# Retention after softplus and squared-ReLU products: each tile's retention moved next to its use, the weights' sign taken on ScalarE, and another cut of the first product's tiles

## The chip, the cores and the metric

One core of a Trainium2 chip runs the whole program. The metric is device time in microseconds; the kernel before took 913.0 us (median of 3 runs, 912.48 to 913.43).

## What is computed

Retention (a masked, decayed product of scores with v), and on its output two feed-forward layers, the first with softplus, the second with a squared ReLU. All inputs and results are float32, and the weights come as float64.

```python
scores = scale * np.matmul(q, k.transpose(0, 1, 3, 2))        # batch 4, heads 8, sequence 576, head 64
ret = scores * Dmat[None]                                     # gamma ** (row - column), causal
x = np.matmul(ret, v)  ->  [2304 tokens, 512]
h = x @ w_in;  x = (np.maximum(h, 0) + np.log1p(np.exp(-np.abs(h)))) @ w_out    # 512 -> 2048 -> 512
h = x @ w_in2; out = np.maximum(h, 0) ** 2 @ w_out2                             # 512 -> 2048 -> 512
```

## The kernel before

Every float32 operand of the large products is split into two parts, hi and lo, and a product is three passes (hi by hi, hi by lo, lo by hi). So one step of a layer, 128 of its 2048 inner columns over one tile of tokens, is 12 matmuls of the first product (`g1`, line 336, tile `ph`) and 12 (in the second phase three per 128 tokens) of the second (`g2`, line 405, tile `acc`). A block is one tile of tokens, 16 steps; `g2` runs two steps behind `g1`. The first phase (softplus) has five blocks, whose lengths in tokens stand in `TILES` (line 25: 512 and four times 448); the second phase (squared ReLU) has five, in `TILES2` (line 26: 384, 512, 512, 512, 384). In the first phase the tokens are the moving columns of both products; in the second they are the moving columns of `g1` alone, and `g2` moves 512 weight columns.

Softplus per step: three ScalarE operations (lines 350 to 352) and three on VectorE (357, 360, 363), then the split of its result (383 on ScalarE, 384 on VectorE).

The weights are split on the chip, one item per 128 rows or columns of a weight matrix (`split_w`, lines 108 to 141): 32 items a phase. An item waits for its load (512 KB, lines 100 and 105, into one of three stages), takes two ScalarE operations (121, 122), a VectorE operation that isolates the sign (126), one that puts the words together (130, tile `ct`), a ScalarE copy to hi (138) and a VectorE subtraction to lo (139). `weights(j)` says how many items are to be through by step j: all 32 of the first phase within the 16 steps of block 0. The other 32 are split in blocks 4 and 5. `pump_step` runs one piece of an item's split, up to the next `yield`; while the first tile is prepared, each chunk calls it once.

The retention runs in 36 chunks of 64 tokens, every chunk a tick: scores and state (`step_s`, lines 237 and 243, then the mask on VectorE at 247 and a state copy on ScalarE at 249), and one tick later the output (`step_o`, line 259, then the decay weights on VectorE at 275). v is weighted on VectorE at line 222 (`scale_v`). The chunks are loaded four ahead (208, 212). Chunks 0 to 7 make the first tile before block 0 starts. The other 28 are spread evenly over the first 29 steps by `attend`, half a tick at the start and half at the end of a step. The output of chunks of tile 1 stays on chip in `x_raw`; that of later tiles goes to device memory (`x1d`, line 285) and comes back a block ahead (line 428). At the end of a block `split_x` (316 to 319) makes the next tile's hi and lo.

Only the start is ordered by hand (`manual_schedule`). After it the order of instructions on each engine comes from a planner that takes the program's order as priority and moves work that is ready ahead of work that waits. Loads and stores are all issued by SyncE's queue, in order.

Of the kernel before, what the change touches and what calls it, by code (L numbers as in the profile page):

```python
# [16 lines left out]
P = 128  # L17
D = 64
CN = 64  # tokens of a chunk of the retention
SCN = 9  # chunks of a sequence  # L20
LOADS = 4  # chunks on chip
STAGES = 3  # weights on chip as they come
XEND = 29  # steps of the first product that carry the retention
# Tiles of tokens of the two phases: start, length.
TILES = ((0, 512), (512, 448), (960, 448), (1408, 448), (1856, 448))
TILES2 = ((0, 384), (384, 512), (896, 512), (1408, 512), (1920, 384))
# Columns of the constants' array: 1 - 2^-23, 0.49, weights of v, the causal mask (the latter two in the
# lower half of the partitions), and weights of the output.
# [6 lines left out]
def kernel(  # L35
# [12 lines left out]
    """Products of float32 matrices as three passes: each operand is the exact sum of two parts  # L48
    that float32r holds, hi (rounded) and lo (the rest), and hi*hi, hi*lo and lo*hi are summed in
    PSUM; lo*lo lies below float32's last bit.  # L50

    Retention runs in chunks of 64 tokens, with every head in the free dimension. Two operands are
    stacked in the partitions: [q, transposed; masked scores] against [state; v] gives a chunk's
    output. With i counted from the sequence's start, v takes gamma^-i, and the output scale *
    gamma^i; the state, the sum of k * v over the chunks before, then grows in PSUM without decay.
    """
# [32 lines left out]
    x1d = [dram.tile([P, n // CN, KD, CN], F32, name=f"x1d{t}") for t, (_, n) in enumerate(TILES)]  # L89
    x2d = dram.tile([KD, P, NT], F32, name="x2d")  # L90

    # ---------------------------------------------------------------- weights
# [15 lines left out]
    def split_w(phase, kind, f):  # L108
        """The two words of each float64 to float32 hi and lo, in steps.

        2^-112 times the upper word, read as a float32, has float32's exponent in place of
        float64's (values below float32's range go to 0). Shifted by 3 bits, with the sign put back
        and with 3 bits for the lower word, it is the float32. The lower word's upper half is
        mapped to 0 to 7, which keeps the mean error at 0.
        """
        t = staged.pop((kind, f))
        y, up, low = t.bitcast(F32)[:, :, 1], t[:, :, 1], t[:, :, 0]
        ct = cvt.tile([P, DM], U32, tag="ct", name="ct")
        halves = t.bitcast(U16).rearrange("p a (b two) -> p a b two", two=2)
        half, sign = halves[:, :, 0, 1], halves[:, :, 1, 1]  # L120
        nc.scalar.activation(out=y, in_=y, func=AF.Copy, scale=2.0**-112)
        nc.scalar.activation(
            out=low, in_=half, func=AF.Identity, bias=round_up, scale=7.0 / 65535
        )
        yield
        nc.vector.tensor_scalar(  # L126
            out=half, in0=sign, scalar1=0x8000, scalar2=None, op0=ALU.bitwise_and
        )
        yield
        nc.vector.scalar_tensor_tensor(  # L130
            out=ct, in0=up, scalar=3, in1=low,
            op0=ALU.logical_shift_left, op1=ALU.bitwise_or,
        )
        yield
        y = ct.bitcast(F32)
        hi = wts.tile([P, DM], F32R, tag=f"{kind}h{f}", name=f"{kind}h{f}")
        lo = wts.tile([P, DM], F32R, tag=f"{kind}l{f}", name=f"{kind}l{f}")
        nc.scalar.copy(hi, y)
        nc.vector.tensor_tensor(out=lo, in0=y, in1=hi, op=ALU.subtract)  # L139
        w_hi[phase, kind, f], w_lo[phase, kind, f] = hi, lo  # L140
        yield True
# [19 lines left out]
    def pump_step():  # L161
        """A step of the next weights' split; loads others into the stage that a whole one frees."""
        if not splitting:
            m = n_split[0]
            if m == len(items):
                return
            pump_load(m + 1)
            splitting.append(split_w(items[m][0], items[m][2], items[m][3]))
            n_split[0] += 1
        if next(splitting[0]):  # L170
            splitting.clear()
            pump_load(n_split[0] + STAGES)

    def pump(count):
        """Splits the next weights."""
        for _ in range(count):
            while True:
                pump_step()
                if not splitting:
                    break  # L180

    # -------------------------------------------------------------- retention
# [45 lines left out]
    def step_s(c, split):  # L228
        """Scores of chunk c, with keys in the partitions, and the state after it."""
# [6 lines left out]
        for h in range(H):  # L236
            nc.tensor.matmul(  # L237
                pb[HI, h, :], lhsT=kk[LO, h, :], rhs=qp[LO, h, :],
                start=True, stop=True, skip_group_check=True,
            )  # L240
            if go_on:
                # One start clears what the whole bank held.
                nc.tensor.matmul(
                    st[LO, h, :], lhsT=kk[HI, h, :], rhs=sv[HI, h, :],
                    start=c % SCH == 0 and h == 0, stop=True, skip_group_check=True,
                )
# [4 lines left out]
    def step_o(c, ps):  # L251
# [16 lines left out]
        elif t == 1:  # L268
            if t not in x_raw:
                x_raw[t] = xs.tile([P, 512 // CN, KD, CN], F32, tag="xr", name="xr")  # L270
            x = x_raw[t][:, m]
        else:
            # In place of the chunk's keys, which nothing reads any more.
            x = qkv[:, 1, 0:KD, :]
        nc.vector.tensor_tensor(out=x, in0=po, in1=xw, op=ALU.mult)
        if t == 0:
            # Nothing reads the operands of a product yet.
# [6 lines left out]
        if t > 1:  # L284
            nc.sync.dma_start(out=x1d[t][:, m], in_=x)
# [3 lines left out]
    def tick_first(split=False):  # L289
        """Scores and state of chunk k."""  # L290
# [4 lines left out]
    def tick_second(ps_o, load=True):  # L295
        """Output of chunk k - 1; loads run ahead."""
# [7 lines left out]
    # ------------------------------------------------------------------ GEMMs  # L304
    def split_x(raw, phase, n):
        """raw -> a tile's operands of the first product."""
# [34 lines left out]
    def softplus_a(key, n):  # L341
        """e = exp(-|h|), ln(1 + e), and a bound of log1p(e) from below that is sharp for small e.

        1 + e is rounded, which spoils the logarithm of small e: it is taken a last bit lower, and
        e - e^2/2 takes over where that is more.
        """
# [76 lines left out]
    def load_x(phase, t0, n):  # L423
        raw = xs.tile([P, 512 * KD], F32, tag="xr", name="xr")
        if phase == 0:
            t, _ = tile_of(t0)
            raw = raw.rearrange("p (m a b) -> p m a b", a=KD, b=CN)
            nc.sync.dma_start(out=raw[:, :n // CN], in_=x1d[t])
        else:
            raw = raw.rearrange("p (a b) -> p a b", a=KD)  # L430
            nc.sync.dma_start(
                out=raw[:, :, :n], in_=x2d[:, :, t0:t0 + n].rearrange("k p n -> p k n")
            )
        return raw

    # --------------------------------------------------------------- schedule
# [3 lines left out]
    # Chunks that have to be through before each tile of the first phase.  # L440
# [9 lines left out]
    def keep_warm(count):  # L450
        """Products that nothing reads: TensorE's clock stays up while the operands come."""
# [36 lines left out]
    half = [0]  # L488
    rest = 2 * (NCH - need[0])

    def attend(j, h2):
        """Attention's half ticks, spread evenly over the first steps."""
        pos = 2 * j + h2 + 1
        want = min(rest, -(-rest * pos // (2 * XEND)))
        while half[0] < want:
            if half[0] % 2 == 0:
                tick_first()
            else:
                tick_second(ps_at)
                scale_v(tick[0] - 2 + LOADS)  # L500
            half[0] += 1

    def weights(j):
        """How many weights of the first phase are split by step j."""
# [10 lines left out]
    for j, (b, f) in enumerate(steps):  # L515
# [11 lines left out]
        attend(j, 0)  # L527
        if j >= 1:
            split_g(j - 1, blocks[steps[j - 1][0]][2])
        if ph == 0:  # L530
            pump(max(0, weights(j) - n_split[0]))
        if j >= 2:
# [5 lines left out]
        attend(j, 1)  # L538
# [8 lines left out]
        if f == KF - 1 and b + 1 < len(blocks):  # L547
            split_x(x_next[0] if b else x_raw.pop(1), blocks[b + 1][0], blocks[b + 1][2])
            if b + 2 < len(blocks):
                x_next[0] = load_x(*blocks[b + 2])  # L550
# [11 lines left out]
def _by_dims(a):  # L562
    """[B, H, S, D] -> chunk, dimension, head, token of the chunk."""
# [7 lines left out]
def _by_tokens(a):  # L571
    """[B, H, S, D] -> chunk, token of the chunk, head, dimension."""
# [7 lines left out]
def _constants(n_heads, head_dim):  # L580
    """Decay weights and the causal mask: they depend on shapes alone."""
# [48 lines left out]
```

## Time and profile before

| | |
|---|---|
| time, 3 runs | 912.48, 913.0, 913.43 us; median 913.0 us |
| profiled execution, span | 913.3 us (no other time of it is recorded) |
| TensorE matmul / weight load busy | 896.1 us (98%) / 765.7 us (84%) |
| VectorE, ScalarE, GpSimd busy | 517.6 (57%), 429.3 (47%), 12.3 us (1%) |
| mean granted TensorE clock | 0.992 of full speed |
| moved by DMA | 74.2 MB, 81 GB/s over the span |

Matmuls overlap, so a matmul's own duration in the trace is longer than its share of the time; what counts is the distance from one start to the next. The clock was full (1.00, that is 2.4 GHz) in every stretch after the start. Engines' busy shares are given by stretch below, since the stages have different limits.

### The profile page before, as it was taken

The page shows a single profiled execution, that of the slowest core. Times are in us where ns is not written, and L with a number is a line of the kernel's source. Part 1 is how long each engine was busy: PE and PEld are TensorE (multiplying, and loading weights), DVE is VectorE, ACT ScalarE, POOL GpSimd, SP SyncE. Part 2 cuts the span into 40 slices and gives each one's busy share as a digit, 9 for nine tenths or more (in the row PEclk, how much of TensorE's full clock was granted, in tenths as well). Part 3 has the DMA queues.
Part 4 walks back from the last instruction along what each step waited for, and adds up shares of the span by engine and source line. Part 5 has one row for each costly group of instructions (what it writes and reads, how often), then busy time and mean ns, then how long its engine had stood idle before and what let it go on. Part 6 is the DMA issues. An engine that isn't in the chain of part 4 may idle for free.

```text
span 913.3 us, 13514 instructions
## 1 busy us (share of the span) xinstructions
PE 896.1 (98%) x5478; PEld 765.7 (84%) x5478; DVE 517.6 (57%) x849; ACT 429.3 (47%) x751; POOL 12.3 (1%) x16
## 2 busy tenths in 40 slices
PE   7999999999999999999999999999999999999998
PEld 6876777788899999999999998888888888888997
DVE  2799999966555547456985799522332233223322
ACT  2588777643454455444875598322222222222222
POOL 2300000000000000000000000000000000000000
PEclk8899999999999999999999999999999999999999
DMA  9867577743111002001520465200020001000100
GB/s 247 202 168 234 163 217 206 216 119 88 42 47 41 0 1 81 1 1 36 179 93 0 156 206 164 81 1 0 1 93 1 1 22 59 1 1 1 46 1 35
DMA packets 39181, 74.20 MB, mean 81 GB/s; under 512 B 3280, under 2 KB 25552, under 8 KB 38992
## 3 DMA queue, kind: packets, MB, share of 16 engines
q1 hardware_dynamic: 39120, 73.35, 26.7%
q8 instruction: 43, 0.70, 0.3%
q14 instruction: 18, 0.15, 0.1%
HBM read 61.15 MB, written 12.19 MB: 80 GB/s over the span
## 4 chain that ended last, share of the span: by engine, by line
PE 77%; DVE 10%; DMA 8%; ACT 3%; issue 2%; SPq 0%; POOL 0%; POOLq 0%; ACTq 0%; DVEq 0%
PE acc L405 37%; PE ph L336 36%; DMA wi_raw<-in_moe_w_in_dram 4%; DVE ct L130 2%; DMA wo_raw<-in_moe_w_out_dram 2%; DMA ch<-in_kv_dram 1%; PE po L259 1%; PE st L237 1%; DVE wo_raw L126 1%; DVE wol L139 1%; DVE wil L139 1%; DVE gl L384 1%; PE cold L453 1%; DVE wi_raw L126 1%; DVE l L360 1%
## 5 line engine op out<-in xcount | busy, mean ns | idle before, releaser
L336 PE MATMUL ph<-xh,wih 128*128 128x512 f32 (+2 forms) x640 | 240.3, 376 | 1.3 <-ACT xh L279 0.4
L336 PE MATMUL ph<-xh,wil 128*128 128x512 f32 (+2 forms) x640 | 238.0, 372 | 0.3 <-DVE wil L139 0.3
L336 PE MATMUL ph<-xl,wih 128*128 128x512 f32 (+2 forms) x640 | 159.0, 370 | 0.0
L336 PEld LDWEIGHTS ph<-xh,wih 128*128 128x128 f32 x640 | 120.2, 188 | 20.2 <-DVE xh L318 1.0
L336 PEld LDWEIGHTS ph<-xh,wil 128*128 128x128 f32 x640 | 120.3, 188 | 16.0 <-DVE wil L139 0.8
L336 PEld LDWEIGHTS ph<-xl,wih 128*128 128x128 f32 x640 | 118.8, 188 | 14.8
L405 PE MATMUL acc<-gh,woh 128*128 128x448 f32 (+1 forms) x320 | 121.4, 381 | 0.0
L405 PE MATMUL acc<-gl,woh 128*128 128x448 f32 (+1 forms) x320 | 119.6, 374 | 0.3 <-DVE gl L384 0.2
L405 PE MATMUL acc<-gh,wol 128*128 128x448 f32 (+1 forms) x320 | 119.7, 374 | 0.0
L376 DVE TENSOR_TENSOR g<-r 128x512 f32<-128x512 f32 (+1 forms) x80 | 51.2, 639 | 114.3 <-ACT r L370 111.7
L405 PE MATMUL acc<-woh,gl 128*128 128x512 f32 x288 | 113.1, 393 | 1.0 <-DVE gl L384 1.0
L405 PE MATMUL acc<-wol,gh 128*128 128x512 f32 x288 | 112.7, 391 | 0.0
L405 PE MATMUL acc<-woh,gh 128*128 128x512 f32 x288 | 112.3, 390 | 0.0
L384 DVE TENSOR_TENSOR gl<-g,gh 128x512 fp32r<-128x512 f32 (+1 forms) x80 | 51.1, 639 | 102.0 <-ACT gh L383 102.0
L370 ACT ACTIVATE r<-ph 128x512 f32<-128x512 f32 (+1 forms) x80 | 44.2, 553 | 129.5 <-PE ph L336 129.5
L383 ACT CAST gh<-e 128x448 fp32r<-128x448 f32 (+1 forms) x80 | 46.0, 575 | 119.5 <-DVE e L363 117.2
L383 ACT CAST gh<-g 128x512 fp32r<-128x512 f32 (+1 forms) x80 | 46.3, 579 | 116.0 <-PE acc L405 107.1
L357 DVE SCALAR_TENSOR_TENSOR e<-e 128x448 f32<-128x448 f32 (+1 forms) x80 | 51.3, 641 | 65.7 <-ACT l L352 65.4
L384 DVE TENSOR_TENSOR gl<-e,gh 128x448 fp32r<-128x448 f32 (+1 forms) x80 | 51.1, 639 | 30.4 <-ACT gh L383 29.9
L405 PEld LDWEIGHTS acc<-gh,woh 128*128 128x128 f32 x320 | 60.1, 188 | 8.2
L405 PEld LDWEIGHTS acc<-gl,woh 128*128 128x128 f32 x320 | 60.1, 188 | 7.5 <-DVE gl L384 1.0
L405 PEld LDWEIGHTS acc<-gh,wol 128*128 128x128 f32 x320 | 60.1, 188 | 7.5
(52 smaller groups left out, 1068.9 us busy)
## 6 DMA issues: line engine op xcount, KB each, us to landing
wi_raw<-in_moe_w_in_dram SPq DMA_DIRECT2D x32, 512.0 KB, 4.6
wo_raw<-in_moe_w_out_dram SPq DMA_DIRECT2D x32, 512.0 KB, 3.9
ch<-in_qk_t_dram SPq DMA_DIRECT2D x36, 256.0 KB, 4.9
ch<-in_kv_dram SPq DMA_DIRECT2D x36, 256.0 KB, 5.4
out_dram<-xo SPq DMA_DIRECT2D x18, 256.0 KB, 2.0
x2d<-xo SPq DMA_DIRECT2D x16, 224.0 KB, 2.0
xr<-x2d SPq DMA_DIRECT2D x3, 1024.0 KB, 5.0
x1d<-ch SPq DMA_DIRECT2D x21, 128.0 KB, 2.3
```

The costliest lines, as they stand in the source:

```text
L126: nc.vector.tensor_scalar(out=half, in0=sign, scalar1=0x8000, scalar2=None, op0=ALU.bitwise_and)
L130: nc.vector.scalar_tensor_tensor(out=ct, in0=up, scalar=3, in1=low, op0=ALU.logical_shift_left, op1=ALU.bitwise_or,)
L139: nc.vector.tensor_tensor(out=lo, in0=y, in1=hi, op=ALU.subtract)
L237: nc.tensor.matmul(pb[HI, h, :], lhsT=kk[LO, h, :], rhs=qp[LO, h, :], start=True, stop=True, skip_group_check=True,)
L259: nc.tensor.matmul(po[(LO, HI)[h % 2], h // 2, :], lhsT=sv[rows, h, :], rhs=qp[rows, h, :], start=True, stop=True, skip_group_check=True,)
L336: nc.tensor.matmul(ph[:, :n], lhsT=a, rhs=x, start=(j == 0), stop=(j == len(todo) - 1))
L357: nc.vector.scalar_tensor_tensor(out=e, in0=e, scalar=-2.0, in1=e, op0=ALU.add, op1=ALU.mult)
L370: nc.scalar.activation(out=r, in_=hps.pop(key)[:, :n], func=AF.Relu)
L376: nc.vector.tensor_tensor(out=g, in0=r, in1=r, op=ALU.mult)
L383: nc.scalar.copy(h[:, :n], g)
L384: nc.vector.tensor_tensor(out=l[:, :n], in0=g, in1=h[:, :n], op=ALU.subtract)
L405: nc.tensor.matmul(o, lhsT=a, rhs=x, start=(begin and m == 0), stop=(end and m == 2))
```

## The change

The tiles of the first phase become 512, 384, 512, 512, 384. The sign operation on VectorE goes; in its place line 121's ScalarE operation is a parametric ReLU in place of a copy: negative values are multiplied by -2^32 more, which sets the bit of the exponent field that the later shift moves into the sign's place. An item's split has three pieces instead of four. The retention of tile b + 1 now runs during block b, whole ticks (the output of one chunk, then scores and state of the next), spread over the first 15 of its 16 steps, after that step's weights. Its output is written to `x_raw`, and nothing goes through `x1d` any more.

```diff
-XEND = 29  # steps of the first product that carry the retention
-TILES = ((0, 512), (512, 448), (960, 448), (1408, 448), (1856, 448))
+TILES = ((0, 512), (512, 384), (896, 512), (1408, 512), (1920, 384))
...
-        nc.scalar.activation(out=y, in_=y, func=AF.Copy, scale=2.0**-112)
+        nc.scalar.activation(out=y, in_=y, func=AF.Prelu, scale=2.0**-112, alpha=-(2.0**32))
...
-        yield
-        nc.vector.tensor_scalar(
-            out=half, in0=sign, scalar1=0x8000, scalar2=None, op0=ALU.bitwise_and
-        )
...
-        elif t == 1:
+        else:
             if t not in x_raw:
                 x_raw[t] = xs.tile([P, 512 // CN, KD, CN], F32, tag="xr", name="xr")
             x = x_raw[t][:, m]
-        else:
-            x = qkv[:, 1, 0:KD, :]
...
-        if t > 1:
-            nc.sync.dma_start(out=x1d[t][:, m], in_=x)
...
+    def attend(b, f):
+        if b < last_b:
+            before, n = need[b], need[b + 1] - need[b]
+            while tick[0] - 1 - before < min(n, -(-n * (f + 1) // (KF - 1))):
+                c = tick[0]
+                step_o(c - 1, ps_at)
+                load_chunk(c - 1 + LOADS)
+                if c < NCH:
+                    step_s(c, False)
+                scale_v(c - 1 + LOADS)
+                tick[0] += 1
...
-        attend(j, 0)
         if j >= 1:
             split_g(j - 1, blocks[steps[j - 1][0]][2])
         if ph == 0:
             pump(max(0, weights(j) - n_split[0]))
+        if ph == 0:
+            attend(b, f)
...
-        attend(j, 1)
...
-            split_x(x_next[0] if b else x_raw.pop(1), blocks[b + 1][0], blocks[b + 1][2])
-            if b + 2 < len(blocks):
-                x_next[0] = load_x(*blocks[b + 2])
+            split_x(x_next[0] if b >= last_b else x_raw.pop(b + 1), *blocks[b + 1][::2])
+            if last_b <= b + 1 < len(blocks) - 1:
+                x_next[0] = load_x(*blocks[b + 2][1:])
```

## Rows read from the trace of the kernel before

**Rows 1.** The page: the span, and the engines' busy time over it.
```profile
span 913.3 us, 13514 instructions
PE 896.1 (98%) x5478; PEld 765.7 (84%) x5478; DVE 517.6 (57%) x849; ACT 429.3 (47%) x751; POOL 12.3 (1%) x16
```
**Rows 2.** Timeline of PE, first matmul of blocks 0, 1 and 5: start us, us.
```profile
39.20 0.50 PE L336 MATMUL ph<-xh,wih 128*128 128x512 f32 x1 [0.40 <-ACT xh L279]
...
163.28 0.47 PE L336 MATMUL ph<-xh,wih 128*128 128x448 f32 x1
...
506.85 0.34 PE L336 MATMUL ph<-xh,wih 128*128 128x384 f32 x1
```
**Rows 3.** Busy time by stretch (blocks 0, 1, 5): PE, PEld, DVE, ACT, POOL, clock, DMA.
```profile
39.20:163.30 124.10, 119.01 (x1097) 90.54 (x1097) 119.78 (x196) 99.02 (x169) 0.00 (x0) 1.00 0.71 201
163.30:268.80 105.50, 104.96 (x914) 88.47 (x914) 71.44 (x120) 48.63 (x84) 0.00 (x0) 1.00 0.33 95
...
506.90:577.10 70.20, 69.01 (x343) 61.35 (x342) 60.55 (x104) 52.45 (x96) 0.00 (x0) 1.00 0.53 171
```
**Rows 4.** The chain that ended last, in order of time: start us, us, what.
```profile
200.53 2.63 PE ph L336 x12
203.17 0.62 PE po L259 x16
203.78 2.63 PE acc L405 x12
...
241.40 1.07 PE st L237 x16
...
278.86 2.48 PE ph L336 x12
...
592.23 2.72 PE ph L336 x12
```
**Rows 5.** Busy groups of block 0 (39.2 to 163.3 us), VectorE and ScalarE: count, busy, mean.
```profile
L126 DVE TENSOR_SCALAR wo_raw<-wo_raw 128x512 uint16<-128x512 uint16 x16 | 12.2, 765 | 0.0
...
L247 DVE TENSOR_TENSOR ch<-st,cst 64x512 f32<-64x512 f32 x16 | 11.1, 695 | 0.9 <-PE st L243 0.3 <-issue 0.2
L222 DVE TENSOR_TENSOR ch<-ch,cst 64x512 f32<-64x512 f32 x16 | 11.0, 688 | 0.4
...
L126 DVE TENSOR_SCALAR wi_raw<-wi_raw 128x512 uint16<-128x512 uint16 x13 | 9.8, 753 | 0.1
...
L249 ACT COPY ch<-st 64x512 f32<-64x512 f32 x14 | 8.1, 575 | 3.0 <-DVE ch L247 2.7
```
**Rows 6.** The same groups: ScalarE's two first operations of an item.
```profile
L122 ACT ACTIVATE wo_raw<-wo_raw,cst 128x512 uint32<-128x512 uint16 x16 | 12.2, 763 | 0.0
...
L121 ACT ACTIVATE wo_raw<-wo_raw 128x512 f32<-128x512 f32 x16 | 10.8, 674 | 4.5 <-DMA wo_raw<-in_moe_w_out_dram 4.5
```
**Rows 7.** Timeline of PE: a 384-column `g1` of block 9 and what follows it.
```profile
841.73 0.33 PE L336 MATMUL ph<-xh,wih 128*128 128x384 f32 x1
...
843.83 0.39 PE L405 MATMUL acc<-woh,gh 128*128 128x512 f32 x1
```
**Rows 8.** Timeline of PE: two neighbours of a 512-column `g2` of block 0.
```profile
165.36 0.39 PE L405 MATMUL acc<-gh,wol 128*128 128x512 f32 x1
165.59 0.39 PE L405 MATMUL acc<-gh,woh 128*128 128x512 f32 x1
```
**Rows 9.** Waits of block 0, and the chain there: one load.
```profile
ACT wi_raw L121 <- DMA wi_raw<-in_moe_w_in_dram: 6.0, 5, 1.5
...
86.80 6.87 DMA wi_raw<-in_moe_w_in_dram
```
**Rows 10.** Busy time by stretch, 20 us of block 5 (columns as in Rows 3).
```profile
540.00:560.00 20.00, 19.82 (x100) 17.68 (x99) 19.00 (x32) 17.48 (x33) 0.00 (x0) 1.00 0.65 197
```
**Rows 11.** Waits of 506 to 600 us: total us, times, longest.
```profile
PEld acc L405 <- DVE gl L384: 2.1, 3, 1.1
```
**Rows 12.** All groups: the one table load of ScalarE.
```profile
L445 ACT ACT_TABLE_LOAD x1 | 1.3, 1283 | 0.7 <-PEq L606 0.7
```

More of the change, by code (lines that the diff above doesn't have):

```diff
@@ L88 @@
     mask = cst[CN:P, C_MASK:C_MASK + CN].unsqueeze(1).to_broadcast([CN, H, CN])
-    x1d = [dram.tile([P, n // CN, KD, CN], F32, name=f"x1d{t}") for t, (_, n) in enumerate(TILES)]
     x2d = dram.tile([KD, P, NT], F32, name="x2d")
@@ L119, in split_w @@
         halves = t.bitcast(U16).rearrange("p a (b two) -> p a b two", two=2)
-        half, sign = halves[:, :, 0, 1], halves[:, :, 1, 1]
-        nc.scalar.activation(out=y, in_=y, func=AF.Copy, scale=2.0**-112)
+        half = halves[:, :, 0, 1]
+        nc.scalar.activation(out=y, in_=y, func=AF.Prelu, scale=2.0**-112, alpha=-(2.0**32))
         nc.scalar.activation(
             out=low, in_=half, func=AF.Identity, bias=round_up, scale=7.0 / 65535
-        )
-        yield
-        nc.vector.tensor_scalar(
-            out=half, in0=sign, scalar1=0x8000, scalar2=None, op0=ALU.bitwise_and
         )
@@ L421, in drain, with load_x @@
                 nc.sync.dma_start(out=out[t0 + j * P:t0 + (j + 1) * P, :], in_=o)
[L423 to L433, printed above, removed]
+    def load_x(t0, n):
+        raw = xs.tile([P, KD, 512], F32, tag="xr", name="xr")
+        nc.sync.dma_start(
+            out=raw[:, :, :n], in_=x2d[:, :, t0:t0 + n].rearrange("k p n -> p k n")
+        )
         return raw
@@ L486 @@
     tick[0] += 1
[L488 to L501, printed above, removed]
+    def attend(b, f):
[9 more added lines that the diff above has]
+                tick[0] += 1
     def weights(j):
```

## The prediction

> **What bounds the kernel now.** I read the page first: TensorE is busy 98% of a span of 913.3 us [rows 1]. That average hides the stages, so I next looked for where each block starts [rows 2] and took the busy time between those marks [rows 3]. Blocks 2 to 4 need no row of their own: their step is 4.96 us (24 matmuls at the pace of the 448-column row, 2.48 us for 12, [rows 4]), a block 79.4 us, and three of them counted back from 506.85 put the end of block 1 at 268.8. So the span is 39.2 (start) + 124.1 (block 0) + 105.5 (block 1) + 238.1 (blocks 2 to 4) + 406.4 (second phase).
>
> In block 0 VectorE is busy 119.8 of 124.1 us, 97%, and ScalarE 80% [rows 3]: VectorE is the bound there. TensorE looks busy too, but its work alone would take less. From the chain: 12 matmuls take 2.48 us at 448 columns and 2.72 us at 512; a step with a tick of the retention reads 2.63 + 0.62 + 2.63 + 1.07 us, about 2.0 us over the bare 4.96 [rows 4]. Block 0 has 16 steps of 5.44 and 15.4 ticks, 117.9 us; it lost some 6 us to VectorE. Everywhere later TensorE itself is the bound, and only fewer or cheaper matmul slots shorten it.
>
> **The tiles.** 448 columns cost 2.48/12 = 207 ns, 512 cost 227 ns [rows 4], and the 384-column `g1` of block 9 goes from 841.73 to 843.83, 2.10 us or 175 ns a matmul [rows 7]. From 175 to 227 over 128 columns is 0.406 ns a column; on that line 448 would cost 201 ns. So 448 carries 6 ns too much. Four blocks of 448 take 317.4 us; two of 512 (2 x 16 x 5.44 = 174.1) and two of 384 (2 x 16 x 4.20 = 134.4) take 308.5. That is **-9.0 us** of TensorE time, with nothing beside it to eat it. The value for 384 is taken from the second phase, where it alternates with 512; that first-phase matmuls pace alike is seen for 512 in block 0 (165.36 to 165.59, 0.23 us, [rows 8]). The bounds are 0 (384 pays the 6 ns as well) and -9.
>
> Here a rule speaks against the change. The Trainium skill (TensorE: Matmul & The Clock Gate, "Back-to-back issue gap") gives a warm matmul's gap as columns over 2.4 GHz plus a constant 2.5 ns. By it two tiles of 448 and a pair of 512 and 384 cost the same, and the total below would be 9 us higher. The trace disagrees at 448, where 207 ns stand against 189.
>
> **The ticks.** Their number stays: 28. A half tick inserted among the large matmuls lengthens the group behind it from 2.48 to 2.63 us [rows 4], and there are two such places in a tick now. With the output and the scores side by side there may be one, which gives 1.85 us instead of 2.0; if the planner parts them, 2.0 stays. I take 1.9, so 28 x 0.1 = **-2.8 us** (bounds 0 and -4.2).
>
> **Block 0.** VectorE loses 29 sign operations, 12.2 + 9.8 = 22.0 us, and 10 of 16 ticks (6 remain) of 0.695 + 0.688 us [rows 5] and about 0.42 us at line 275, which is 18.0 us: 119.8 falls to about 80. ScalarE loses 8 state copies of 0.575 us [rows 5], 99.0 to 94.4. TensorE needs 16 x 5.44 + 6 x 1.9 = 98.4 us. So the bound passes to TensorE, with ScalarE close behind at 96% of that. ScalarE waits in order, for loads (6.0 us for one of the two kinds, [rows 9]), and those waits do not go. On the other hand block 5 shows 20 us in which VectorE had 95%, ScalarE 87% and TensorE still 99% [rows 10]. I take 104 us: 98.4 from TensorE and 5.6 for ScalarE's waits, which is 94.4 + 10 seen from ScalarE.
>
> Parametric ReLU has no row. Its operand and shape are those of the copy, 674 ns; the other operation of an item, with a per-partition operand, takes 763 [rows 6]. I take 674, since scale and slope are constants as before; at 763 ScalarE gets 30 x 0.09 = 2.7 us more in block 0. A gain is excluded, since only the function changes and a copy is the simplest there is.
>
> **Blocks 1 to 4.** Block 1: 67.2 + 8 ticks x 1.9 = 82.4. Block 2: 87.0 + 15.2 = 102.2. Block 3: 87.0 + 6 x 1.9 = 98.4. Block 4: 67.2. VectorE and ScalarE were at 68% and 46% in block 1 with 12.6 ticks [rows 3], so 8 ticks over a block stay covered. The first output written to `x_raw` in a block waits until `split_x` has read the old one; behind it on VectorE stand the mask and that step's softplus. As `split_x` runs on VectorE ahead of it anyway, I price this at nothing; without that cover it is one split, some 0.6 us, at three boundaries. The last chunk is through one step before its tile is split, so that is covered by one step of TensorE.
>
> **Queues.** 21 stores and 3 loads of `x1d` go, all beside other work since no TensorE wait names them. A chunk's two loads now stand behind that step's weight loads in SyncE's queue; a chunk loaded is used three ticks later, in block 0 some 48 us, so this costs nothing. In the start the shorter item lets the third item begin and puts the fourth item's load ahead of chunk 8's; chunk 8 is not in the first tile. I price it at 0, between -1 and +2 us (512 KB at the 201 GB/s of [rows 3] is 2.6 us).
>
> **The second phase.** Block 5's first two `g2` are of 384 columns instead of 448: -0.8 us. Block 5's 16 steps would take about 67.8 us and took 70.2, with VectorE at 60.6 and TensorE waiting for its `gl` [rows 3, 11]. The sign operations leave there, but ScalarE stays at 52.5 of 70; I give half of the 2.4 us back, -1.2. So 404.4.
>
> **The sum.** 39.2 + 104 + 82.4 + 102.2 + 98.4 + 67.2 + 404.4 = 897.8 us of span. The profiled execution's span is 0.3 us over the median of 913.0, so I forecast **897.5 us**, 15.5 less than before: 9.0 from the tiles, 2.8 from ticks, 2.0 from the second phase, and the rest from the loss in blocks 0 and 1. What this kernel's runs can tell from no change is 0.2%, 1.8 us.
>
> **Rivals.** First, *the tiles give nothing*: the 6 ns of a 448-column matmul would be the first phase's, not the shape's. For it: all 448 rows lie in the first phase, and 384 is never seen there. Against it: 512 in block 0 carries none [rows 8]. Time: 906.5.
>
> Second, *the weights' cycle binds block 0*. Three stages serve 30 items; a load that took 6.87 us [rows 9], ScalarE's 1.44, VectorE's 0.69 and some 2 us of queueing make 11 us for three items, 3.7 a piece, 110 us in all, and up to 115 where chunk loads collide. For it: ScalarE's waits for loads. Against it: block 5 ran at 197 GB/s [rows 10], 2.6 us an item. Time: 904 to 909, at 907.
>
> Third, the other side: *parametric ReLU is not in the table that ScalarE holds*, and each item then switches tables twice. One table load takes 1283 ns [rows 12]: 30 x 2.57 = 77 us on ScalarE in block 0, 171 us in place of 104, and some 35 us in block 5; about 1,000 us. It decides from 0.85 us more an item, where ScalarE would reach 120 us in block 0 and eat the whole 15.5. For it: the trace shows no such function. Against it: one table served six functions (absolute value, exponential, logarithm, copy, identity, ReLU) with a single load in all 751 instructions. The Trainium skill (ScalarE: Activation LUTs, "Table sets: the hidden batching unit") says that cheap functions are in every set and names ReLU, copy, identity and absolute value; the parametric form is not named, and no run here shows it.
>
> **How the numbers follow.** The forecast, 890 to 902: 0.62. The tiles give nothing: 0.10. The weights' cycle: 0.16. The table: 0.03. A better case, in which ScalarE's waits are covered in block 0 and the ticks cost 1.85, below 890: 0.09. The range from 888 to 909 holds the first three and a part of the last; it leaves out the table and ends beyond these. Faster by over 0.2% come all but the table and a little of what is not named: 0.94; within 0.2%: 0.02; slower: 0.04.
>
> **What would show it.** Right: block 0 of 101 to 107 us with VectorE near 80; `po` and `st` next to each other in the chain; first-phase 384 rows of 2.1 us for 12; no second table load; block 1 near 82. Wrong: 384 rows at 2.17 or more for 12; ScalarE over 95% in block 0 with waits for loads above 15 us; the start well over 39.2.

## The result, and the profile after

The changed kernel takes 896.75 us (median of 4 runs, 895.3 to 898.63), the kernel before 912.99 in the same runs: a ratio of 0.9821, with a 95% interval of 0.9803 to 0.9839. The forecast was 897.5.

With the result every run's span is known beside its time: the time is 1.95 to 2.1 us longer in the four runs of the changed kernel, and 2.1 to 2.2 in all runs of before beside the experiments. The profiled execution after has a span of 893.2 and a time of 895.3; the one before, whose span of 913.3 the sum was made against, therefore took some 915.4 (an estimate) and not the 913.0 that the prediction set beside it. So the stages below, one execution each, add up to 20.1 us less, where the medians differ by 16.2: before's execution was some 2.4 us above its median, after's 1.5 below. A difference of 1 or 2 us between stages of two kernels can be that of two executions.

The page after: span, busy time by engine, and the chain by engine (`g1` is now line 326, `g2` line 395).

```profile
span 893.2 us, 13363 instructions
PE 878.4 (98%) x5478; PEld 756.2 (85%) x5478; DVE 480.6 (54%) x785; ACT 425.2 (48%) x751; POOL 12.1 (1%) x16
...
PE 93%; DMA 2%; ACT 2%; DVE 1%; issue 0%; POOL 0%; SPq 0%; POOLq 0%; DVEq 0%
```

The page's chain of before:

```profile
PE 77%; DVE 10%; DMA 8%; ACT 3%; issue 2%; SPq 0%; POOL 0%; POOLq 0%; ACTq 0%; DVEq 0%
```

TensorE had 77% of it, VectorE 10% and DMA 8%. Now the chain is TensorE's nearly from end to end. Busy time by stretch after, cut where each block's first `g1` starts; columns as in [rows 3]. The first row is the start, the second block 0, the third block 1, the last block 5.

```profile
0.00:41.00 41.00, 31.70 (x480) 27.67 (x480) 16.10 (x27) 13.67 (x26) 12.10 (x16) 0.92 0.90 230
41.00:138.80 97.80, 97.03 (x639) 77.82 (x640) 89.09 (x144) 89.92 (x160) 0.00 (x0) 0.98 0.69 202
138.80:222.20 83.40, 83.20 (x753) 78.87 (x752) 55.76 (x100) 43.11 (x82) 0.00 (x0) 1.00 0.23 64
...
489.40:556.30 66.90, 66.90 (x344) 61.40 (x343) 50.46 (x88) 51.70 (x97) 0.00 (x0) 1.00 0.56 177
```

Block 0 went from 124.1 to 97.8 us and VectorE in it from 119.8 to 89.1; ScalarE stands at 89.9, so that all three engines are at 91% or more. In the timeline's block starts, stage by stage (us of span):

| | start | block 0 | block 1 | block 2 | block 3 | block 4 | second phase | span |
|---|---|---|---|---|---|---|---|---|
| before | 39.2 | 124.1 | 105.5 | 79.4 | 79.4 | 79.4 | 406.4 | 913.3 |
| forecast | 39.2 | 104 | 82.4 | 102.2 | 98.4 | 67.2 | 404.4 | 897.8 |
| after | 41.0 | 97.75 | 83.5 | 101.2 | 97.6 | 68.4 | 403.8 | 893.2 |

The chain of block 1 after, in order of time: start us, us, what. Two steps, one bare and one with a tick.

```profile
185.48 2.08 PE acc L395 x12
187.56 2.08 PE ph L326 x12
189.64 0.62 PE po L254 x16
190.26 0.20 PE st L232
...
191.34 2.28 PE acc L395 x12
193.62 2.08 PE ph L326 x12
195.70 2.08 PE acc L395 x12
```

Twelve matmuls of 384 columns take 2.08 us in the first phase too (rows 7 had 2.10). Output and scores stand side by side, only the group behind them is longer (2.28), and from `ph` at 187.56 to `ph` at 197.78 two steps take 10.22 us, 1.90 over two bare ones: the tick costs what the forecast took. The rows of ScalarE's parametric ReLU on one of the two kinds of items, and of its table load, over the whole execution:

```profile
L120 ACT ACTIVATE wi_raw<-wi_raw 128x512 f32<-128x512 f32 x32 | 21.4, 669 | 5.3 <-DMA wi_raw<-in_moe_w_in_dram 5.1
L429 ACT ACT_TABLE_LOAD x1 | 1.3, 1283 | 0.7 <-PEq L589 0.7
```

The parametric ReLU takes 669 ns, the copy took 674 [rows 6], and there is one table load as before: the third rival is out. The Trainium skill (ScalarE: Activation LUTs, "Table sets: the hidden batching unit") says that cheap functions appear in every set; this run shows that the parametric form behaves so in the set loaded here.

### The profile page after: what moved, and what is told of

It reads as the page before. It is cut to its first block, busy times and chain, and to the rows that moved or that the text cites. A ratio compares the mean times of both kernels' runs of the same rounds, so it can differ in the third digit from the quotient of the medians.

```text
span 893.2 us, 13363 instructions
## 1 busy us (share of the span) xinstructions
PE 878.4 (98%) x5478; PEld 756.2 (85%) x5478; DVE 480.6 (54%) x785; ACT 425.2 (48%) x751; POOL 12.1 (1%) x16
## 4 chain that ended last, share of the span: by engine, by line
PE 93%; DMA 2%; ACT 2%; DVE 1%; issue 0%; POOL 0%; SPq 0%; POOLq 0%; DVEq 0%
PE ph L326 43%; PE acc L395 43%; PE st L232 3%; PE po L254 2%; DMA ch<-in_kv_dram 1%; PE st L238 1%; DMA wi_raw<-in_moe_w_in_dram 1%; PE cold L437 1%; DMA cst<-in_consts_dram 0%; PE pb L232 0%; DVE wil L134 0%; POOL ch L217 0%; DVE ct L125 0%; ACT wi_raw L120 0%; ACT e L341 0%
## 5 line engine op out<-in xcount | busy, mean ns | idle before, releaser
L326 PE MATMUL ph<-xh,wih 128*128 128x512 f32 (+1 forms) x640 | 236.9, 370 | 1.3 <-ACT xh L271 0.9
L326 PE MATMUL ph<-xh,wil 128*128 128x512 f32 (+1 forms) x640 | 236.9, 370 | 0.0
L326 PE MATMUL ph<-xl,wih 128*128 128x512 f32 (+1 forms) x640 | 157.6, 368 | 0.0
L395 PE MATMUL acc<-gh,woh 128*128 128x512 f32 (+1 forms) x320 | 120.7, 377 | 0.0
L395 PE MATMUL acc<-gh,wol 128*128 128x512 f32 (+1 forms) x320 | 117.8, 368 | 0.0
L395 PE MATMUL acc<-gl,woh 128*128 128x512 f32 (+1 forms) x320 | 117.7, 368 | 0.0
L373 ACT CAST gh<-g 128x512 fp32r<-128x512 f32 (+1 forms) x80 | 46.2, 578 | 115.3 <-PE acc L395 105.9
L373 ACT CAST gh<-e 128x512 fp32r<-128x512 f32 (+1 forms) x80 | 46.0, 574 | 104.7 <-DVE e L353 77.5
L347 DVE SCALAR_TENSOR_TENSOR e<-e 128x512 f32<-128x512 f32 (+1 forms) x80 | 51.1, 638 | 66.2 <-ACT l L342 65.5
L374 DVE TENSOR_TENSOR gl<-e,gh 128x512 fp32r<-128x512 f32 (+1 forms) x80 | 51.0, 638 | 36.9 <-ACT gh L373 36.4
L340 ACT ACTIVATE e<-ph 128x512 f32<-128x512 f32 (+1 forms) x80 | 44.1, 551 | 51.7 <-PE ph L326 50.9
```

Of the source, the lines that this page charges most:

```text
L326: nc.tensor.matmul(ph[:, :n], lhsT=a, rhs=x, start=(j == 0), stop=(j == len(todo) - 1))
L340: nc.scalar.activation(out=e, in_=ph[:, :n], func=AF.Abs)
L347: nc.vector.scalar_tensor_tensor(out=e, in0=e, scalar=-2.0, in1=e, op0=ALU.add, op1=ALU.mult)
L373: nc.scalar.copy(h[:, :n], g)
L374: nc.vector.tensor_tensor(out=l[:, :n], in0=g, in1=h[:, :n], op=ALU.subtract)
L395: nc.tensor.matmul(o, lhsT=a, rhs=x, start=(begin and m == 0), stop=(end and m == 2))
```

## Experiments

The change has three parts, so six kernels hold one or two of them each, and with before and after the eight combinations are complete. Five more test single steps, and one repeats the changed kernel. The table gives the stages of each kernel's profiled execution (us of span; "rest" is from block 6 on), its median time and its ratio to the runs of before on the same chip.

| kernel | start | block 0 | block 1 | blocks 2-4 | block 5 | rest | median us | ratio (95%) |
|---|---|---|---|---|---|---|---|---|
| before | 39.2 | 124.1 | 105.5 | 238.1 | 70.3 | 336.2 | 912.99 | 1 |
| tiles_only | 38.5 | 124.9 | 94.1 | 243.3 | 68.2 | 336.6 | 907.83 | 0.9936 (0.9921-0.9951) |
| sign_only | 41.5 | 118.2 | 103.9 | 238.1 | 68.0 | 336.2 | 906.9 | 0.9924 (0.9909-0.9939) |
| ret_only | 38.3 | 113.0 | 91.4 | 259.7 | 70.3 | 336.2 | 910.7 | 0.9973 (0.9961-0.9985) |
| sign_back | 39.0 | 108.1 | 82.4 | 268.4 | 68.7 | 336.2 | 904.92 | 0.9901 (0.9881-0.992) |
| tiles_back | 40.3 | 103.3 | 91.5 | 260.6 | 69.5 | 336.3 | 904.46 | 0.9907 (0.9878-0.9935) |
| ret_back | 41.5 | 115.6 | 92.9 | 241.5 | 66.9 | 336.1 | 898.26 | 0.9824 (0.9798-0.9851) |
| after | 41.0 | 97.8 | 83.5 | 267.2 | 66.9 | 336.9 | 896.75 | 0.9821 (0.9803-0.9839) |
| after_again | 43.6 | 96.7 | 83.0 | 267.2 | 66.9 | 336.9 | 897.25 | 0.9826 (0.9801-0.9851) |
| ticks_parted | 40.4 | 101.6 | 85.4 | 270.0 | 66.9 | 336.8 | 905.39 | 0.9903 (0.9875-0.9931) |
| four_pieces | 38.1 | 98.6 | 84.4 | 267.1 | 67.9 | 336.2 | 895.67 | 0.981 (0.9775-0.9844) |
| hi_on_vector | 40.1 | 105.1 | 84.8 | 268.0 | 68.3 | 336.2 | 903.92 | 0.9891 (0.9864-0.9919) |
| merged_early | 41.9 | 115.0 | 89.5 | 241.5 | 66.9 | 336.1 | 893.07 | 0.9781 (0.9763-0.98) |
| merged_early_start | 40.8 | 113.7 | 90.9 | 242.2 | 70.6 | 336.1 | 892.21 | 0.9775 (0.9752-0.9797) |

### One part alone

**tiles_only.** The kernel before with the one line changed:

```diff
-TILES = ((0, 512), (512, 448), (960, 448), (1408, 448), (1856, 448))
+TILES = ((0, 512), (512, 384), (896, 512), (1408, 512), (1920, 384))
```

> The kernel before with the new tiles of the first phase alone. Theory (a 448-column matmul carries 6 ns too much): blocks 1 to 4 lose 9 us of TensorE time between them, block 0 stays at about 124 us, so about 904 us. Rival (a matmul's time goes linearly with its columns): no change, 913.

Measured: 907.83, some 6 us less (0.64% of 913; 4.5 to 7.2 by the interval). Blocks 1 to 5 together took 405.5 us instead of 413.8, 8.3 less, while block 0 stayed. So the linear rule falls: the cut is worth time. In plain steps the cut is worth even 10 us (a step reads 4.96 us at 448 columns, 5.44 at 512 and 4.16 at 384). Some 2 us are paid back in block 4, which is now shorter and still splits weights with the sign operation (70.3 us where after has 68.4).

**sign_only.** The kernel before with line 121's function exchanged and the sign operation gone:

```diff
-        nc.scalar.activation(out=y, in_=y, func=AF.Copy, scale=2.0**-112)
+        nc.scalar.activation(out=y, in_=y, func=AF.Prelu, scale=2.0**-112, alpha=-(2.0**32))
...
-        yield
-        nc.vector.tensor_scalar(
-            out=half, in0=sign, scalar1=0x8000, scalar2=None, op0=ALU.bitwise_and
-        )
```

> The kernel before with the parametric ReLU and without the sign operation on VectorE. Theory (block 0 was bound by VectorE): VectorE's busy time in block 0 falls from 120 to about 100 us, TensorE's floor there with 15.4 ticks is 112.5 us (the first two steps have no second product), so block 0 takes about 115 to 117 us instead of 124, and block 5 loses its 2.4 us: about 903 us. Rival (table switches): table loads beside the first, over 960 us. Rival (ScalarE binds instead): block 0 stays at 120 or more, 910.

Measured: 906.9. Block 0 took 118.2 us, and it became TensorE's. Its busy time by stretch (columns as in [rows 3]):

```profile
41.50:159.60 118.10, 117.56 (x1086) 91.33 (x1086) 107.98 (x175) 99.93 (x173) 0.00 (x0) 0.98 0.76 213
```

The chain in the middle of it:

```profile
99.86 2.94 PE ph L332 x12
102.81 1.07 PE st L233 x16
103.88 2.95 PE acc L401 x12
106.83 0.61 PE po L255 x16
107.44 2.94 PE ph L332 x12
```

From the third on nearly every step is 7.58 us without a gap: 5.44 and a parted tick of 2.14, because both groups behind an insertion read 2.94 where bare ones read 2.72. Of the 118.2, some 2.5 us lie in the first step, which ran at the low clock (6.1 us; 3.6 in ret_back, whose block 0 is otherwise the same and took 115.6). VectorE fell to 108.0, not to 100: 29 operations of 0.76 us are gone, and its busy time is only 11.8 us less. Two things take up the rest. The block now ends with six operations of the next tile's split on VectorE (3.7 us) that lay behind it before, so that the durations in the block fell by 17 us and not by 22. And durations overlap: those of block 0 before add up to 132 us in 119.8 busy, here to 115.5 in 108.0. Block 5 lost its 2.3 us. But the start grew by 2.3, which neither theory had (four_pieces, below).

**ret_only.** The kernel before with the change's `attend` and `x_raw`, the old tiles and the sign operation (the diff ahead of the prediction without its first two parts).

> The kernel before with the retention moved next to its use and kept on chip, old tiles, sign operation on VectorE. Theory (a tick moved out of block 0 saves VectorE time there and costs TensorE time later): block 0 is still bound by VectorE at about 109 to 113 us, 11 to 15 less than before, but 9.4 ticks of 1.9 us come back in blocks 1 to 3, so in all -2 to +6 us: about 915. Rival (the parts add up: what the change gained is shared by the parts, some 5 us of it here): 908.

Measured: 910.7, only 2.5 us less. Block 0 lost 11 us, as the theory had it, and blocks 1 to 4 gained 7.5, as ticks that had been free beside VectorE's work now cost TensorE time. The theory wanted more back: with tiles of 448 some 8 ticks (not 9.4) move to later blocks, 15 us at 1.9. Most of the difference lies in the pace of 448 columns, which is not one number, and in cheaper ticks. The chain of this kernel, before and after a switch in the middle of a plain stretch:

```profile
453.77 2.48 PE ph L330 x12
456.25 2.48 PE acc L399 x12
458.73 2.44 PE ph L330 x12
461.17 2.44 PE acc L399 x12
463.60 2.43 PE ph L330 x12
```

Blocks 1 to 3 mostly run at 2.43 here, 203 ns a matmul, and block 4 from its eighth step; at 0.09 us a step that is some 5 of the 64 steps' possible 5.8 us. What makes 448 columns go at 203 or at 207 ns was not found.

### One part taken out

**sign_back.** The changed kernel with the sign operation and the copy put back.

> The changed kernel with the sign operation put back on VectorE. Theory: VectorE's busy time in block 0 rises from 89 to about 109 us and binds it at about 112 us instead of 98, block 5 gets its 2.4 us back: about 912 us. Rival (VectorE has slack now, at 89 of 98 us, and the operation is mostly covered): block 0 at 102 to 104, 903 us.

Measured: 904.92, 8 us more than after. Block 0 took 108.1 us, of which VectorE was busy 105.9, by the busy time of that stretch:

```profile
39.00:147.10 108.10, 99.36 (x687) 77.73 (x688) 105.89 (x174) 92.68 (x160) 0.00 (x0) 1.00 0.65 190
```

TensorE now waits for softplus on VectorE, as the largest sum among the block's waits says (total us, times, longest):

```profile
PE ph L330 <- DVE e L357: 6.7, 6, 2.3
```

VectorE binds, as the theory said, but busy for 106 us and not 109, and the block takes 108.1 and not 112; the start is 2 us shorter besides. The rival's 903 is nearer in time, but its block of 102 to 104 us did not come; the theory is right in the mechanism. Against the changed kernel 21.9 us of sign operations are back in the block, and VectorE's busy time is 16.8 us longer.

**tiles_back.** The changed kernel with the old `TILES` line.

> The changed kernel with the old tiles (512 and four times 448). Theory: blocks 1 to 4 get 9 us longer, block 0 stays at about 98: about 906 us. Rival (linear in columns): 897.

Measured: 904.46 (902.42 to 911.78), 7.7 more than after. In the profiles block 0 (7 ticks now instead of 6, and more lost) takes 5.6 us of it and block 5 2.6; blocks 1 to 4, mostly at the faster 448 pace of 4.87 us a step and with one tick fewer, only 1.5. So the new cut is worth nearly what was forecast, but not where it was forecast. Why block 0 loses more with the old cut was not tried; a stretch at the low clock, some 1.7 us dearer, lies in block 0 of both executions (in after's first step, here at 137.3 to 140.7 us), so it isn't that.

**ret_back.** The changed kernel with the old `attend`, the old targets of the retention's output and the stores and loads of `x1d`.

> The changed kernel with the old retention (spread over 29 steps, later tiles through device memory); new tiles and parametric ReLU stay. Theory (without the sign operation VectorE no longer binds block 0, so where the ticks lie hardly matters): block 0 about 115 to 117 us, block 1 about 92, blocks 2 to 4 without ticks; only the merged ticks (2.8 us) and a remainder of a few us in block 0 are lost: about 900 us. Rival (moving the ticks was a large part of the gain): 905 or more.

Measured: 898.26, ratio 0.9824 against 0.9821 and 0.9826 for the changed kernel: moving the retention and keeping it on chip adds nothing that can be measured to the other two parts. Block 0 is 115.6, as expected. The reason can be read from the stages: whole ticks save 0.21 us each (6.27 to 6.06 us a step with a tick at 384 columns, 7.59 to 7.38 at 512; 28 of them: 6 us), and block 0 gives about 4 of it back. With 15.4 ticks in block 0 only 0.8 us was lost over TensorE's own slots (81.6 + 15.4 x 2.15 = 114.7); with 6 ticks 4.7 us (81.6 + 6 x 1.9 = 93.0 against 97.75), of which some 1.6 are the low clock in the first step.

### Single steps

**ticks_parted.** In the changed kernel each tick has its two places again:

```diff
-                if c < NCH:
-                    step_s(c, False)
-                scale_v(c - 1 + LOADS)
+                due.append(c)
...
             relu2_b(j, n)
+        attend_second()
```

> The changed kernel with each tick in two places of its step again: output ahead of the second product, scores and state at the step's end. Theory (a place costs 0.15 us): 28 times 0.1 to 0.15, 3 to 4 us more: about 900 us. Rival (what lies between is only the planner's order, and a place costs nothing): 897.

Measured: 905.39, 8.6 more. In the chain both places lengthen the group behind them:

```profile
194.23 0.62 PE po L254 x16
194.84 2.28 PE acc L395 x12
197.13 0.20 PE st L232
...
198.21 2.28 PE ph L326 x12
```

So a place costs 0.20 us, not 0.15, and both the theory's 900 and the rival's 897 are missed. Blocks 1 to 3 grew by 4.9 us for 22 ticks, which is about that price. Block 0 grew by 3.9 for 6 ticks, three times as much; why was not tried.

**four_pieces.** The changed kernel with one more piece, an empty one, in each item's split:

```diff
         yield
+        yield
         nc.vector.scalar_tensor_tensor(
```

> The changed kernel with an empty fourth piece in each item's split, so that the start issues the same pieces at the same chunks as before. Theory (the start grew from 39.2 to 41.0 us, and TensorE fell to the lower clock at its end, because the third item starts there and the fourth item's load stands ahead of chunk 8): start back at 39 us, about 2 to 4 us less in all, 893 to 895. Rival (executions of the same program differ that much in the start): no change, 897.

Measured: 895.67; the runs (893.98 to 898.26) overlap those of after, so the time settles nothing. The start does: 38.1 us, and over all profiles the six kernels with four pieces start block 0 at 38.1 to 40.8 us (39.0 on average), the eight with three at 40.1 to 43.6 (41.3). The clock in the start differs too: TensorE had 6.8 us of it at 1.2 GHz in eight of these profiles, 10 to 17 us in the others. Among those eight, the four with four pieces start at 38.1 to 39.0 and the four with three at 40.1 to 41.5, so the pieces are worth some 2.2 us by themselves. In the changed kernel TensorE waits at the start's end, then its clock falls, and the matmuls of the first product start 430 ns apart (41.37 to 41.80). Its timeline there:

```profile
39.57 0.56 PE L254 MATMUL po<-ch 128*64 128x64 f32 x10 [1.42 <-POOL ch L217]
41.01 0.57 PE L326 MATMUL ph<-xh,wih 128*128 128x512 f32 x1 [0.88 <-ACT xh L271]
41.37 0.63 PE L326 MATMUL ph<-xh,wil 128*128 128x512 f32 x1
41.80 0.63 PE L326 MATMUL ph<-xh,wih 128*128 128x512 f32 x1
```

After's busy time in steps of 2 us there:

```profile
40.00:42.00 2.00, 1.12 (x7) 0.83 (x4) 0.91 (x3) 1.45 (x3) 0.00 (x0) 0.83 1.04 244
42.00:44.00 2.00, 2.00 (x7) 1.54 (x6) 1.78 (x3) 2.00 (x5) 0.00 (x0) 0.50 1.10 246
44.00:46.00 2.00, 2.00 (x13) 1.35 (x12) 0.76 (x2) 0.79 (x2) 0.00 (x0) 0.82 0.88 272
```

A granted clock of 0.50 is the level of 1.2 GHz. The first step read 5.2 us in four of the eight three-piece profiles, 6.1 in sign_only, 3.6 in the other three, where the clock was full, and 3.8 or 3.9 in every four-piece one. So the low clock costs some 1.6 us there.

**after_again.** The changed kernel, unedited, beside the next three.

> The changed kernel once more, unedited, beside the next three on the same chip. Both theories: its time again, 896 to 898 us, with a start of 40.5 to 41.5 us and a block 0 of 97 to 99 us.

Measured: 897.25 (894.5 to 899.98). Its start was 43.6 us, over 2 us longer than expected, and its first step 3.6: this time the clock was full at the start's end, but it had been at 1.2 GHz for longer before, in all of this stretch (columns as in [rows 3]):

```profile
21.30:34.90 13.60, 11.73 (x137) 10.12 (x136) 6.06 (x8) 4.26 (x9) 5.06 (x5) 0.50 0.80 191
```

In after that stretch was half as long, 6.8 us. The two executions of this program differ in the start, block 0 (97.75 and 96.7) and the first step of block 1, and nowhere else by more than 0.1 us. That the times' scatter of 5 us comes from there is likely, but the other runs left no trace.

**hi_on_vector.** In the changed kernel, the copy to hi of the second matrix's items:

```diff
-        nc.scalar.copy(hi, y)
+        if phase == 0 and kind == "wo":
+            nc.vector.tensor_copy(hi, y)
+        else:
+            nc.scalar.copy(hi, y)
```

> The changed kernel with the copy to hi of the second matrix's items of the first phase on VectorE instead of ScalarE. Theory (ScalarE paces block 0's first eight steps at 6.3 to 6.6 us: 2.55 us of softplus and two items of 2.05): ScalarE loses 0.3 us a step there, those steps fall to about 6.0 us, block 0 to about 95 to 96 us, 895 us in all. Rival (the loads pace these steps): no change, 897; and if VectorE binds in its place, block 0 at 98 to 102.

Measured: 903.92, 6.7 more. The theory falls: the second and third step kept their 6.1 to 6.3 us, and ScalarE, with less to do, now waits for loads (11 us; 1.0 in after's block 0), and TensorE for VectorE. The block took 105.1 us, more than any of the forecasts. Its waits from 40 to 142 us (total us, times, longest):

```profile
ACT wi_raw L120 <- DMA wi_raw<-in_moe_w_in_dram: 6.3, 3, 2.4
...
PE ph L329 <- DVE e L356: 4.0, 4, 1.6
...
ACT wo_raw L120 <- DMA wo_raw<-in_moe_w_out_dram: 4.9, 5, 1.6
```

VectorE, at 91% of after's block 0, had little room for more. Whether ScalarE or the loads pace the first steps of after stays open, and also whether either does: TensorE was busy for 97.03 of the 97.80 us of that block.

**merged_early.** The old spread over 29 steps and the way through device memory, with new tiles, parametric ReLU and whole ticks:

```diff
...
+    def attend(j):
+        want = min(NCH - need[0], -(-(NCH - need[0]) * (j + 1) // XEND))
+        while tick[0] - 1 - last < want:
+            c = tick[0]
+            step_o(c - 1, ps_at)
+            load_chunk(c - 1 + LOADS)
+            if c < NCH:
+                step_s(c, False)
+            scale_v(c - 1 + LOADS)
+            tick[0] += 1
...
-        attend(j, 0)
...
+            attend(j)
...
-        attend(j, 1)
```

> New tiles and parametric ReLU with the old spread of the retention over 29 steps and the way through device memory, but each tick whole, in one place after the step's weights. Theory (the moved retention gained by merging the ticks, and lost some 4 us in block 0, where ScalarE paces the first steps at 6.3 to 6.6 us and a tick on TensorE is covered): block 0 at 81.6 + 15.4 times 1.9 + 1 = 112 us, start 41, blocks 1 to 4 with 12.6 ticks at 1.9: about 893 us. Rival (keeping the retention on chip and late is what gains): 897 or more.

Measured: 893.07, all four runs within 892.64 to 893.85, 4.2 less than the changed kernel beside it. The time is as expected; block 0 is 3 us longer than the sum (some 1.6 of them the clock in its first step) and block 1 shorter. After its first three steps block 0 is TensorE's without a gap, 7.38 us a step:

```profile
105.64 2.72 PE ph L332 x12
108.36 0.62 PE po L255 x16
...
110.05 2.97 PE acc L401 x12
113.02 2.72 PE ph L332 x12
```

**merged_early_start.** The same with the empty fourth piece.

> The kernel of the run before, with an empty fourth piece in each item's split. Theory (three pieces lengthen the start by 2 to 3 us and let TensorE's clock fall at its end): start 38 to 39.5 us in place of 40.5 to 41.5, about 891 us. Rival (what the start gives is given back while block 0's first steps wait for their weights): 893.

Measured: 892.21 (890.35 to 896.12), not told apart from 893.07. The profiled execution is the slowest of these. Its start is 1 us shorter (40.8, not the expected 38 to 39.5; 13.7 us of it at the low clock) and its first step 3.8, but block 5 takes 70.6 in place of 66.9, with one wait of 1.6 us for ScalarE's `gh` and then 3.4 us at the low clock. Whether the piece does that isn't shown: four_pieces, with the same piece, took 67.9 there. As the median goes it is the fastest kernel of the study, 2.2% below before.

## Why the forecast held, point by point

**The bound.** Right: block 0 was VectorE's, the rest TensorE's. But the loss in block 0 was taken too small. `g2` runs two steps behind, so block 0's first two steps have no second product, and its floor is 5.44 us lower than the prediction's 16 x 5.44: before lost 11.6 us there at the prediction's 2.0 a tick, 9.5 at the 2.14 that sign_only shows, not 6. The same slip made the forecast of 104 too long: 98.4 + 5.6 should have been 93.0 + 5.6 = 98.6, and 97.75 came. That this fits so well is luck, for the 5.6 stood for ScalarE's waits for loads, and those were 1.0 us. What fills the 4.7 us over TensorE's slots is, as far as the trace tells, 1.6 for the low clock in the first step, 0.8 in which TensorE stood idle, and five places more than there are ticks, some 1.1 us, since in the first half of the block the planner cut the small groups up:

```profile
64.53 0.45 PE L254 MATMUL po<-ch 128*64 128x64 f32 x8
...
73.08 0.45 PE L254 MATMUL po<-ch 128*64 128x64 f32 x8
...
77.50 0.45 PE L254 MATMUL po<-ch 128*64 128x64 f32 x6
...
83.84 0.56 PE L254 MATMUL po<-ch 128*64 128x64 f32 x10
```

The remaining 1.2 us stay open. The lag also moves some 1.3 us (two second products at 2.72 us instead of 2.08) from block to block, which explains 83.5, 101.2 and 68.4 against 82.4, 102.2 and 67.2.

**The tiles.** Right in sign, nearly in size. 384 columns go at 173 ns in the first phase, so the first rival is out. The 448-column matmul, which the whole gain rested on, has two paces, 207 and 203 ns. The gain was 6 us alone and 7.7 beside the other parts; the forecast had 9. The Trainium skill (TensorE: Matmul & The Clock Gate, "Back-to-back issue gap") gives the gap of a single warm matmul as columns over 2.4 GHz plus 2.5 ns. An estimate by it is 162, 189 and 216 ns at 384, 448 and 512 columns; the trace has 173, 203 or 207, and 227, and by its equal price tiles_only would have read 913.

**The ticks.** 1.9 us was right for a whole tick in place. What it replaced was dearer than the 2.0 read at 448 columns: 2.14 at 512. So the term of 2.8 us was too small: 28 whole ticks save 6 us against the same kernel with parted ones (ret_back), outside the bound of 4.2.

**Block 0's engines.** VectorE's 80 us was 89.1 and ScalarE's 94.4 was 89.9. The step that failed is subtracting durations from busy time: neighbouring operations overlap, so a removal frees less. VectorE's durations in the block fell from 132.4 to 96.5 us, by 35.9 and not by 40 (of line 222's operations 7 left the block and not 10), and its busy time by 30.8. On ScalarE durations fell by 6.0 us and busy time by 9.1, since what is left there overlaps more. sign_back shows it for one operation: 21.9 us of durations more, 16.8 of busy time.

**Parametric ReLU, queues, second phase.** Right: 669 ns, one table load, no wait behind `x_raw`. Block 5 gave 3.3 us instead of 2.0; its stall went wholly. The sign operation is not all of that stall: tiles_back, which lacks it too, took 1.7 us more there than its slots (66.9 us and 0.8 for two second products of 448 columns).

**The start.** Wrong: priced at 0 with bounds of -1 and +2, it costs 1.8 us in this execution and about 2.3 over all profiles, besides 1.6 in the first step where the clock falls. The prediction looked at the queue and at chunk 8, not at TensorE's wait ahead of the first product. four_pieces shows that the number of pieces does it; which of the moved instructions, was not tried.

**The total.** The span was forecast 4.6 us too long, and 2.4 us between span and time were missing on the other side. With the 1.5 us by which the profiled execution lies below the median, that leaves 0.75. So 897.5 against 896.75 is nearer than its steps deserve. Of its signs of being right, the 384 columns, the table, `po` beside `st` and block 1 came; block 0 (97.75, not 101 to 107) and VectorE (89, not near 80) did not. The second rival (the weights' cycle) did not bind here: ScalarE's waits for loads shrank to 1 us; the 11 us of them in hi_on_vector suggest that it lies not far off.

**What the change's three parts are worth.** Alone: tiles 6, sign 7, retention 2.5 us by the ratios. On top of the other two: tiles 7.7 to 7.9, sign 7.3 to 8.2, retention 0 to 1.5, by the ratios and by the medians. The third part holds a gain (whole ticks) and a loss (ticks taken from a block where they cost less), and merged_early, with the gain alone, is 4.2 us faster than the changed kernel beside it.

## What to carry to other kernels

When a stage is bound by one engine, another engine's work placed there is nearly free; moving it "just ahead of need" into a stage bound by that other engine gives much of the gain back (in ret_only 7.5 of 11 us). Count the floor of a stage with its pipeline's lag, and do not take a removed instruction's duration for the busy time that it frees: here 22 us of durations were worth 17. A small group of another kind among large matmuls costs a toll for each place it is put in, here 0.2 us, so put such groups together.

## Not expected of the hardware

- A 448-column matmul runs at 207 or 203 ns, and the pace can switch inside a plain stretch (2.48 to 2.44 us for 12 at 458.73 of ret_only), while 384 and 512 show one pace each, 173 to 175 and 227 ns.
- Sixteen, 32 or 48 small matmuls lengthen the following group of twelve by 0.20 to 0.25 us (2.08 to 2.28, 2.72 to 2.97).
- After waits of 1.4 and 0.9 us and a thin stretch ahead of them, TensorE's clock fell from 2.4 to 1.2 GHz for some 3.4 us (0.83, 0.50 and 0.82 in the three stretches of 2 us from 40 us on), when it was at full work again; in after_again, with the same program and the same two waits, it was full there and had been low earlier.
